# Q of a windowed attention transposed by DMA and read by the score matmuls as it lies, head by head on 64 rows

## Chip, cores, metric

One core of a Trainium2 chip. The sessions ran on different chips; the kernel before ran in each of them, with medians of 306.8 to 308.1 us, so times of different sessions are compared. The time is device microseconds of an execution; a number given for a kernel is the median of its runs. Ratios are the mean time of one kernel's fast runs over that of the other's fast runs of the same rounds, so they are not quite the ratio of the medians. A run more than 1.5% above the fastest of the same kernel counts as slow.

## The reference

```python
# q, k, v: 8 batches x 8 heads x 576 tokens x 64, values near 0.1; window of 64, causal
scores = q @ k.T / sqrt(64);  keep 0 <= i - j < 64;  attn = softmax(scores);  x = attn @ v
x = x.transpose(0, 2, 1, 3).reshape(4608, 512)
out = (((x @ w1) * (x @ w2)) @ w3) @ w_out          # 512 -> 1024 -> 1024 -> 512
```

The scores are so small that the softmax is nearly uniform over its window. An exchange of queries inside a batch need not be seen by the comparison with the reference.

## The kernel before

A batch has 6 steps, two for each third of 192 queries; a step covers two head pairs. K and Q of a batch are loaded as fp32 (576 tokens as 32 partitions x 18 tokens, for 4 head pairs), cast on POOL, transposed by DMA (at the start by PE), and put in token order by copies on ACT and DVE: K to `kT`, each of Q's two heads to its half of `qT`, whose other half is zero. One score matmul of 128 rows then serves both heads.

```python
    def load_qk(b, which, gate=None):
        ...
        for hh in range(2):
            nc.sync.dma_start(out=t[:, hh], in_=src[b, hh:H:2].rearrange("j (p r) d -> p j (r d)", r=TI))
    ...
    def scores(d):
        ...
                nc.tensor.matmul(s_ps[:, jj, c0:c0 + 2 * n].rearrange("k (a n) -> k a n", a=2),
                                 kT[:, 2 * jp + jj, k0:k0 + P], qT[:, 2 * jp + jj, :, q0:q0 + n], ...)
        nc.scalar.activation(pt[:, :, 0:w], s_ps[:, :, 0:w], AF.Exp, bias=-SHIFT, scale=scale)
        for (lo, hi, n, off, step) in ...:                      # masks, POOL, innermost 128 or 64
            nc.gpsimd.affine_select(out=sl, in_=sl, pattern=pat, compare_op=ALU.is_ge, fill=0.0, ...)
            nc.gpsimd.affine_select(out=sl, in_=sl, pattern=[[-s, m] for s, m in pat], ...)
    ...
    def values(d):
        o_ps = ps_v.tile([P, 2, 512], FP32, name="o_ps")        # one buffer only
        ...                                                     # matmuls, then ACT: Ln, Ln, Exp -> r
        nc.vector.tensor_tensor(xs[0:D], o_ps[0:D, :, 0:192], r[0:D], ALU.mult)
        nc.vector.tensor_tensor(xs[D:P], o_ps[D:P, :, 192:384], r[D:P], ALU.mult)
```

`xs` is a piece of `xT`, the fp16 input of the feed-forward part. V is loaded by casting loads that POOL issues; DVE copies halves of it (`copy_v`).

## Time and profile before

| | before |
|---|---|
| time | 307.23 us (306.78 to 309.35) |
| first scores in the trace | 15.9 us |
| busy PE / DVE / ACT / POOL | 269 / 214 / 191 / 195 us of 306 |
| from one batch's first scores to the next's, us | 39.5, 33.1, 29.9, 29.3, 31.9, 33.9, 27.4 |

The last row is worked out from the start times of the score matmuls. Groups of the profile: line, engine, operation, output and input with their shapes, count, then busy microseconds and mean ns of one, then the idle time before them.

### The profile page before, as it was taken

To read this page: it belongs to the slowest core of one execution; us is meant where nothing else is said; L and a number is where in the kernel's file an instruction comes from. 1 tells how busy PE (TensorE), PEld (TensorE's weight loads), DVE (VectorE), ACT (ScalarE), POOL (GpSimd) and SP (SyncE) were. 2 spreads that over 40 slices of the span, in tenths; PEclk is the share of its full clock that TensorE was granted. 3 is DMA by queue.
4 is the path that set the end of the run, shared out by engine and by line. 5 is a ranking of instruction groups with operands and counts; after the bars stand their busy time and mean duration, and the time that the engine had idled before them with its cause. 6 is when DMAs were issued, how large, how long until landed. Compare 5 with 4: busy or idle time off the path is not lost.

```text
span 306.0 us, 5153 instructions
## 1 busy us (share of the span) xinstructions
PE 269.2 (88%) x1846; PEld 154.0 (50%) x1846; DVE 213.8 (70%) x302; ACT 190.7 (62%) x296; POOL 194.7 (64%) x214
## 2 busy tenths in 40 slices
PE   8598989798477999997899689996999899999992
PEld 8584645444223455554455379553554455554440
DVE  6815687555977678887988877769799766455531
ACT  2423784686285959897689656497769865741310
POOL 9754994578617986899589835695888544320300
PEclk9869999999959999999999999999999999999998
DMA  6999999973774997599679945994179003003012
GB/s 245 203 183 199 299 237 247 351 48 85 183 196 112 320 97 215 89 326 105 164 133 301 113 136 113 330 163 80 23 144 130 0 25 116 0 6 136 0 39 106
DMA packets 79694, 45.88 MB, mean 150 GB/s; under 512 B 66816, under 2 KB 69888, under 8 KB 79664
## 3 DMA queue, kind: packets, MB, share of 16 engines
q0 software_dynamic: 41744, 9.96, 39.5%
q1 hardware_dynamic: 37920, 35.54, 38.9%
q8 instruction: 15, 0.25, 0.4%
q14 instruction: 15, 0.12, 0.2%
HBM read 38.80 MB, written 9.44 MB: 158 GB/s over the span
## 4 chain that ended last, share of the span: by engine, by line
PE 51%; DVE 12%; ACT 11%; issue 8%; DMA 8%; POOL 7%; SPq 1%; DVEq 0%; POOLq 0%; ACTq 0%
PE f_ps L416 24%; PE f_ps L429 12%; DMA v<-in_v_dram 5%; PE o_ps L329 5%; PE tp L500 4%; PE s_ps L294 3%; DVE xT L345 3%; POOL pt L308 3%; ACT qT L274 3%; ACT ln_s L339 2%; DMA stage<-in_q_dram 2%; ACT r L341 2%; DVE kT L274 2%; DVE t2k L431 2%; ACT pt L299 2%
## 5 line engine op out<-in xcount | busy, mean ns | idle before, releaser
L416 PE MATMUL f_ps<-xT,w_sb 128*128 128x512 f16 (+1 forms) x640 | 137.5, 361 | 11.7 <-DVE xT L345 4.4
L308 POOL TENSOR_SCALAR_AFFINE_SELECT pt<-pt 128x512 f16<-128x512 f16 (+1 forms) x64 | 61.2, 956 | 66.7 <-ACT pt L299 66.6
L416 PEld LDWEIGHTS <-w_sb 128*128 128x128 f16 x640 | 61.1, 98 | 65.6 <-issue 17.2
L429 PE MATMUL f_ps<-wc_sb,ab 128*128 128x512 f16 x288 | 67.2, 379 | 0.4
L422 DVE TENSOR_TENSOR ab<-f_ps,a_sb 128x512 f16<-128x512 f32 x72 | 49.5, 690 | 17.7 <-PE f_ps L416 14.6
L299 ACT ACTIVATE pt<-s_ps 128x1024 f16<-128x1024 f32 (+1 forms) x48 | 45.6, 950 | 23.4 <-PE s_ps L294 22.6
L310 POOL TENSOR_SCALAR_AFFINE_SELECT pt<-pt 128x512 f16<-128x512 f16 (+1 forms) x64 | 56.7, 885 | 4.4
L421 ACT COPY a_sb<-f_ps 128x512 f32<-128x512 f32 x72 | 41.5, 578 | 21.6 <-PE f_ps L416 21.4
L344 DVE TENSOR_TENSOR xT<-o_ps,r 64x384 f16<-64x384 f32 x48 | 26.3, 549 | 39.0 <-ACT r L341 38.6
L338 ACT ACTIVATE ln_s<-o_ps 64x384 f32<-64x384 f32 x48 | 23.4, 488 | 41.1 <-PE o_ps L329 40.9
L429 PEld LDWEIGHTS <-ab 128*128 128x128 f16 x288 | 27.5, 98 | 30.2 <-DVE ab L422 1.8
L329 PE MATMUL o_ps<-pt,v 128*128 128x128 f16 (+1 forms) x384 | 28.0, 215 | 11.4 <-DVE xT L345 7.3
L235 POOL DMA_DIRECT2D v<-in_v_dram x40 | 33.9, 855 | 5.4 <-DMA ab<-in_moe_w_out_dram 3.6
L329 PEld LDWEIGHTS <-v 128*128 128x128 f16 x384 | 23.6, 98 | 24.5 <-issue 11.0
L431 DVE COPY t2k<-f_ps 128x512 f32<-128x512 f32 x36 | 24.7, 689 | 9.4 <-PE f_ps L429 8.8
L294 PE MATMUL s_ps<-qT,kT 128*128 128x256 f16 x192 | 28.1, 271 | 2.2 <-ACT qT L274 2.2
L274 ACT COPY qT<-q_tr 64x768 f16<-64x768 f16 x18 | 27.5, 1536 | 3.2 <-DMA q_tr<-q 3.2
L345 DVE TENSOR_TENSOR xT<-o_ps,r 64x384 f16<-64x384 f32 x48 | 26.9, 561 | 0.6
L341 ACT ACTIVATE r<-ln_s 128x384 f32<-128x384 f32 x48 | 25.1, 523 | 1.5
L274 DVE COPY qT<-q_tr 64x768 f16<-64x768 f16 x18 | 23.7, 1323 | 0.5
L294 PEld LDWEIGHTS <-kT 128*128 128x128 f16 x192 | 18.0, 100 | 11.9 <-DVE qT L274 2.2
L339 ACT ACTIVATE ln_s<-o_ps 64x384 f32<-64x384 f32 x48 | 23.2, 483 | 0.6
(65 smaller groups left out, 189.5 us busy)
## 6 DMA issues: line engine op xcount, KB each, us to landing
stage<-in_k_dram SPq DMA_DIRECT2D x16, 576.0 KB
stage<-in_q_dram SPq DMA_DIRECT2D x16, 576.0 KB
out_dram<-t2k SPq DMA_DIRECT2D x36, 256.0 KB
v<-in_v_dram POOLq DMA_DIRECT2D x32, 128.0 KB, 8.3
w_sb<-in_moe_w_dram POOLq DMA_DIRECT2D x4, 512.0 KB, 9.3
ab<-in_moe_w_out_dram POOLq DMA_DIRECT2D x1, 1024.0 KB, 9.9
ab<-in_moe_w_dram POOLq DMA_DIRECT2D x2, 512.0 KB, 12.3
xT<-in_moe_w_dram POOLq DMA_DIRECT2D x2, 512.0 KB, 16.6
```

Source lines behind the costliest of these rows:

```text
L235: nc.gpsimd.dma_start(out=vh[lo:P, c], in_=v[b, :, s0:s0 + P - lo, :].rearrange("h s d -> s h d"))
L274: cp(dst[:, :, :, 6 * c:6 * c + 6], src[part])
L294: nc.tensor.matmul(s_ps[:, jj, c0:c0 + 2 * n].rearrange("k (a n) -> k a n", a=2), kT[:, 2 * jp + jj, k0:k0 + P], qT[:, 2 * jp + jj, :, q0: ...
L299: nc.scalar.activation(pt[:, :, 0:w], s_ps[:, :, 0:w], AF.Exp, bias=-SHIFT, scale=scale)
L308: nc.gpsimd.affine_select(out=sl, in_=sl, pattern=pat, compare_op=ALU.is_ge, fill=0.0, base=off, channel_multiplier=-1)
L310: nc.gpsimd.affine_select(out=sl, in_=sl, pattern=[[-s, m] for s, m in pat], compare_op=ALU.is_ge, fill=0.0, base=63 - off, channel_multip ...
L329: nc.tensor.matmul(o_ps[:, jj, o0:o0 + n], v16[:, si * 2 + bi, j0 + jj, a * D:a * D + P], pt[:, jj, c0 + a * n:c0 + a * n + n], start=firs ...
L345: nc.vector.tensor_tensor(xs[D:P], o_ps[D:P, :, 192:384], r[D:P], ALU.mult)
L416: nc.tensor.matmul(d[:, f * n + c0:f * n + c1], w[:, dc, (fc + f) * P:(fc + f + 1) * P], xT[:, dc, xc:xc + c1 - c0], start=first, stop=(dc ...
L421: act_cp(a_sb[:, 0:nf * n], a_ps[:, 0:nf * n])
L422: nc.vector.tensor_tensor(ab[:, fc:fc + nf, lo:hi], b_ps[:, 0:nf * n].rearrange("p (f n) -> p f n", f=nf), a_sb[:, 0:nf * n].rearrange("p ...
L429: nc.tensor.matmul(o_ps, ab[:, fc, t * P:t * P + P], wc_sb[:, fc, :], start=(fc == 0), stop=(fc == 7))
```

## The change

The intent: K must still be put in order, but Q need not. The DMA's transposed tile is read as it lies, so 24 copies on each of ACT and DVE go, and so do the zero halves. The queries now come in the order (i, p), where token = 16 p + i, and each head has its own matmul on 64 rows. To make runs of 16 tokens fit, 512 tokens of a batch are loaded as 32 x 16 with the head pairs outermost, and the last 64 tokens of all batches come in one extra load. The products must then put the tokens back.

```diff
-    qTs = [const.tile([P, NJ, 2, S], FP16, name=f"qT_{i}") for i in range(2)]
+    qlast = const.tile([P, QI, P], FP16)
...
+                nc.sync.dma_start(out=t[:, hh, 0:QI * D],
+                                  in_=q[b, hh:H:2, 0:TP * QI].rearrange("j (p r) d -> j p (r d)", r=QI))
...
+                for a in range(2):
+                    half = slice(a * D, a * D + D)
+                    rhs = qT[half, :, TP * j + p0:TP * j + p0 + np] if p0 < TP else \
+                        qlast[half, :, 16 * b + 4 * j:16 * b + 4 * j + np]
+                    nc.tensor.matmul(s_ps[:, a, jj, c0:c0 + QI * np].rearrange("k (i p) -> k i p", i=QI),
+                                     kT[half, j, k0:k0 + P], rhs, start=True, stop=True, skip_group_check=True)
...
-                pat = [[0, 2], [step, nb], [0, 2], [1, n]]
+                pat = [[0, 4], [step, nb], [1, QI], [QI, np]]          # np = 8 or 4
...
-        nc.vector.tensor_tensor(xs[0:D], o_ps[0:D, :, 0:192], r[0:D], ALU.mult)
+        xs = xs.rearrange("m j (p i) -> m j i p", i=QI)
+        for a in range(2):
+            half = slice(a * D, a * D + D)
+            nc.vector.tensor_tensor(xs[half],
+                                    o_ps[half, :, a * 192:a * 192 + 192].rearrange("m j (i p) -> m j i p", i=QI),
+                                    r[half].rearrange("m j (i p) -> m j i p", i=QI), ALU.mult)
...                                                                    # start: PE transposed Q of batches 0 and 1 before
+    cast_qk(0, "q", 0, dve_cp)
+    cast_qk(0, "q", 1, act_cp)
+    turn(0, "q")
+    load_qk("last", "q")
```

## The prediction

> **What bounds the kernel now.** I began with the page's busy shares and its 40 slices.
>
> ```profile
> PE 269.2 (88%) x1846; PEld 154.0 (50%) x1846; DVE 213.8 (70%) x302; ACT 190.7 (62%) x296; POOL 194.7 (64%) x214
> ...
> PE   8598989798477999997899689996999899999992
> ...
> POOL 9754994578617986899589835695888544320300
> ```
>
> PE is the bound on average, but it dips in slices 10 to 12 (71 to 91 us of 306), and POOL is at 8 or 9 tenths in several slices up to the 30th. In the busy times by stretch POOL has 25.3 of 30 us in 110 to 140 and 24.9 in the next 30, while PE has 29.9 and 26.8: POOL is the second bound, with little to spare there. The list of waits says what POOL's reserve is, and the chain of work that ended last shows the dip:
>
> ```profile
> POOL pt L308 <- ACT pt L299: 66.6, 25, 8.4
> ```
>
> ```profile
> 85.19 2.65 SPq L252
> 87.89 0.59 SPq L208
> 88.53 6.75 DMA stage<-in_q_dram
> 95.33 1.15 POOL q L216
> 96.47 0.60 POOL pt L308
> ```
>
> 66.6 us is nearly all the time in which POOL waits for work between its first mask and its last. The chain near 90 us runs over a load of Q: POOL, strictly in order, waits in its cast for the load, and the masks stand behind the cast. The groups by shape give what the change removes:
>
> ```profile
> L274 ACT COPY qT<-q_tr 64x768 f16<-64x768 f16 x18 | 27.5, 1536 | 3.2 <-DMA q_tr<-q 3.2
> ...
> L294 PE MATMUL s_ps<-qT,kT 128*128 128x256 f16 x160 | 27.0, 278 | 2.2 <-ACT qT L274 2.2
> ...
> L274 DVE COPY qT<-q_tr 64x768 f16<-64x768 f16 x18 | 23.7, 1323 | 0.5
> ```
>
> Those 51 us of copies are large, but the waits they end are small: 3.2 us on ACT, 2.2 on PE. Last, the timeline of POOL, undisturbed masks:
>
> ```profile
> 1.17 0.29 POOL masks.py:199 TENSOR_SCALAR_AFFINE_SELECT ident<-ident 128x128 f16<-128x128 f16 x1
> ...
> 20.23 0.65 POOL L308 TENSOR_SCALAR_AFFINE_SELECT pt<-pt 128x512 f16<-128x512 f16 x1
> 20.95 0.64 POOL L310 TENSOR_SCALAR_AFFINE_SELECT pt<-pt 128x512 f16<-128x512 f16 x1
> 21.55 0.42 POOL L308 TENSOR_SCALAR_AFFINE_SELECT pt<-pt 128x256 f16<-128x256 f16 x1
> ...
> 31.37 1.12 POOL L310 TENSOR_SCALAR_AFFINE_SELECT pt<-pt 128x1024 f16<-128x1024 f16 x1
> ```
>
> **What the Trainium skill says.** (1) "DMA: Bandwidth & Descriptors", section "Why a DMA increments its semaphore by 16 and not by 1": a DMA runs on the largest k up to 16 that divides the slowest dimension of both sides. Every Q and K load of before has slowest dimensions 32 (source) and 128 (tile), so k = 16; its packets confirm it, with 14.2 in flight on average in the first four loads (2.4 to 9.6 us). (2) "GPSIMD Engine Reference", 3.1: a software loop with a body of up to two operations costs 1.03 cycles per element at 1.2 GHz, 0.86 ns. The trace agrees: its records have 418, 639 and 1,115 ns for undisturbed masks of 256, 512 and 1,024 elements; 639 - 418 = 221 ns over 256 elements is 0.86 ns. (3) "TensorEngine Tiling (Array Packing)", Key Properties: tiles on different rows can run in parallel, and a change of tiling mode drains TensorE. Before has one mode in its matmuls of note, so nothing shows it. (4) "Advanced Engine Details and Errata", Memory Cachelines: access that leaves a line each time is penalized. The trace agrees for SBUF: ACT's 768-element copy takes 1,536 ns from the strided transposed tile and about 800 from PSUM.
>
> **The change part by part.**
>
> *Removed.* ACT: 24 copies to qT, 27.5 + 4.8 (six from PSUM of 0.80) = 32 us. DVE: 24, 23.7 + 5.7 (six of 0.96) = 29 us, and four memsets, 4.1 us, all before 6.2 us when DVE waits for K anyway. PE: 36 transposes of Q, some 2 us, and the waits near 50 us (49.8 to 54.5) in which they, ACT and DVE took turns: 2 to 3 us of path. In the steady batches I give the freed ACT and DVE time 2 to 4 us of path, because PE seldom waits for them.
>
> *Scores and values on PE.* Per score step 4 matmuls of mostly 256 columns on 128 rows become 8 or 12 of 128 or 64 columns on 64 rows (192 to 448 in all). The columns stay 1,024, some 0.44 us in the timeline (start to start of the next group). If the two halves run in parallel it is 0.22 us, at most 48 x 0.22 = 10 us saved; two changes of mode a step, which I guess at 0.1 us each, eat 48 x 0.2 = 10. Values keep their columns (384 to 448 matmuls; the 64-column ones cost about 30 ns start to start) but write PSUM in runs of 4 or 8, point (4). I take PE as neutral, within 5 us. DVE's write of xT, now in steps of 16, may lose part of what DVE gained.
>
> *Masks.* Elements stay equal, instructions go from 128 to 160 (the last third of a batch needs two pairs). But the innermost dimension of the mask's pattern falls from 128 or 64 to 8 or 4. Rows of a pattern per batch before: 4 steps' instructions, 16 each with 4 rows in the first third's two steps (8 instructions, 32 rows) and 8 instructions of 8 rows (64), so 96. After: first third 2 x 4 x 64 = 512, second 2 x 2 x 128 = 512, last 2 x (2 x 64 + 2 x 128) = 768, so 1,792. What a row costs the trace shows only weakly. Take 0.863 ns per element off: 183 ns stay for the identity's mask (1 row), 197 for 256 and 512 elements (4 rows), 232 for 1,024 (8 rows). That is 4.3 ns a row from 1 to 4 and 8.8 from 4 to 8; the mean slope is 49 / 7 = 7 ns, as a software loop that restarts per row would have. Then POOL gains 8 batches x 1,696 rows x 7 ns = 95 us, and 32 instructions x 0.17 = 5 us; casts of Q, 1,152 to 1,024 elements, give back 13 x 0.11 = 1.4 us. POOL's busy time between the first mask (20.2 us) and the last (ends 269.7) is 177 us, so it becomes about 275, more than the 250 us that this stretch now takes: POOL becomes the bound.
>
> *Loads of Q.* The new order puts the four head pairs outermost in the source: slowest dimensions 4 and 128, so k = 4 by point (1). A 4,608-byte packet takes 178 ns in the trace, so one of 4,096 some 158 (estimate); 256 packets on 4 engines are 64 x 158 ns = 10.1 us, where the pair of K and Q loads now lands in 7.2 us together. At the start Q follows K on the same rings, from about 5.5 us, shares its engines with the weights from 8.6 us, and lands near 17 instead of 9.6. Then the casts (1 us) and the transpose: the first one of before was issued at 73.4 and its packets ended at 77.6, so 4.2 us. First scores at about 23 us instead of 15.9; the filler matmuls end near 15.6, so the clock falls and the next 40 fillers run slower, 1 us more. First mask about 25 us. For batch 1, Q lands 6 to 8 us later than its cast is due (now 42.3 and 43.9), another 5 us, less the 3 saved there; at the dip, the load alone takes 10 us instead of 6, another 4. Later loads have 20 us from issue to cast (129.7 and 151.9) and stay hidden.
>
> *Sum.* First mask 25 + POOL's work 275 + 20 us in which it still has none (start, batch 1, the dip) + the tail after the last mask, now 306.0 - 269.7 = 36, partly taken forward by PE's reserve, say 32: 352 us.
>
> **The rivals.** *Rows cost nothing* (the 35 ns between 4 and 8 rows is a matter of 1,024 elements): POOL gains only 5 us, and the time is 307 + 7 to 8 (start) + 2 (batch 1) + 4 (dip) - 6 (copies, scores) = about 314. For it: a straight line through the four durations misses none by over 7 ns. Against: both steps in the rest, 1 to 4 rows and 4 to 8, go up. *The load stays on 16 engines*, and POOL is free as well: start about equal (transpose lands at 16), 4 to 10 us gained, 297 to 303. For it: the filler count of 110 fits a first score at 15.6. Against: the skill's rule is explicit, and Q's order before obeyed it. *PE gets worse*: drains of 0.3 us and slow strided writes would add 48 x 0.5 = 24 us where PE is the bound, 335 with rows free, and hidden behind POOL otherwise. *POOL far worse*: at 12 ns a row 163 us instead of 95, 420.
>
> **Range and chances.** I give a row cost of 4 to 10 ns seven chances in ten: 4 ns leaves POOL just below its bound and makes some 315 to 328 with the loads' terms, 10 ns about 393. Range 312 to 395, middle 352. Faster by over 2% (under 301) needs free rows, 16 engines and overlapping scores: 0.06. Within 2%: 0.09. Slower: 0.85.
>
> **What would show it.** Right: a 512-element mask near 1.1 us instead of 0.64 and a 1,024-element one near 2 instead of 1.12; POOL over 80% busy, PE below 80%; PE's waits for POOL's pt at L308 in tens of us where it is 3.2 now; POOL's wait for ACT shrunk; Q's first load landing after 15 us and the first scores after 20. Wrong: masks of unchanged length, or first scores near 16 us, each of which takes its term out of the sum.

## More of the kernel before

```profile
L345 DVE TENSOR_TENSOR xT<-o_ps,r 64x384 f16<-64x384 f32 x48 | 26.9, 561 | 0.6
L344 DVE TENSOR_TENSOR xT<-o_ps,r 64x384 f16<-64x384 f32 x48 | 26.3, 549 | 39.0 <-ACT r L341 38.6
```

These are the 96 products, 53 us on DVE, 0.55 us each. They read `o_ps`, and until both are done the next step's values cannot start.

## The result

454.85 us (450.99 to 460.12, 4 runs); before 307.34 in the same rounds; ratio 1.474, 95% interval 1.462 to 1.486. The result is right. The direction was predicted, the size was not: 352 was predicted, at most 395. The profile is of the slowest run, 458.3 us of span, which counts as slow (2.0% above the fastest); the three others are 451 to 455, and nothing below rests on that difference. Times read from its trace are some 5 us longer than the median.

The page of the changed kernel, busy times and three of the rows of 40 slices:

```profile
PE 306.9 (67%) x2215; PEld 158.3 (35%) x2215; DVE 298.1 (65%) x274; ACT 163.8 (36%) x273; POOL 299.7 (65%) x246
...
PE   8200665596765809678657765969677768767994
...
DVE  2000167882688545498959996878789897865642
...
POOL 9110469926985449949995999459969977654020
```

PE fell from 88% to 67%, as "PE below 80%" said, but POOL is at 65%, not over 80%: no engine is the bound. POOL is all but idle in slices 2 to 4 (11 to 46 us), where it had work before, and DVE, hardly discussed in the prediction, is as busy as POOL and stays at 8 or 9 tenths over long stretches.

The masks came out as predicted. Timeline of POOL in the changed kernel (start us, us of duration, instruction; in brackets the idle time before it):

```profile
51.49 1.09 POOL L306 TENSOR_SCALAR_AFFINE_SELECT pt<-pt 128x512 f16<-128x512 f16 x1 [24.15 <-ACT pt L295]
...
53.71 0.89 POOL L306 TENSOR_SCALAR_AFFINE_SELECT pt<-pt 128x256 f16<-128x256 f16 x1
...
64.72 2.08 POOL L306 TENSOR_SCALAR_AFFINE_SELECT pt<-pt 128x1024 f16<-128x1024 f16 x1 [3.66 <-ACT pt L295]
```

1.09 us where 0.64 stood for 512 elements, 2.08 where 1.12 stood for 1,024, as announced ("near 1.1", "near 2"). But the first mask comes at 51.5 us (before 20.2), after 24 us of waiting. The products did not come out as predicted. Group of the changed kernel:

```profile
L344 DVE TENSOR_TENSOR xT<-o_ps,r 64x384 f16<-64x384 f32 x96 | 171.8, 1789 | 48.9 <-ACT r L338 48.0
```

The same 96 products, 1,789 ns each instead of 549 and 561: 119 us more on DVE. The list of waits of the changed kernel (waiting instruction, releaser, us in total, times, longest) says where that shows:

```profile
POOL pt L306 <- ACT pt L295: 94.4, 21, 24.1
...
PE o_ps L326 <- DVE xT L344: 49.2, 25, 6.6
...
PE o_ps L326 <- POOL pt L308: 15.7, 6, 9.7
```

The same wait for the products in the kernel before:

```profile
PE o_ps L329 <- DVE xT L345: 7.3, 9, 2.1
```

PE waits 49 us for the products, where it was 7, and less than half of that for the masks, and POOL still waits 94 us for work. A step with little else in it shows the loop: values at 61.70 us, ACT's Ln, Ln, Exp until 63.73, the two products from 63.77 for 3.57 us, the next values at 67.49, so 5.8 us a step. In the kernel before the values of the same stretch start at 30.50 and 33.88, 3.4 us apart.

Last, the start. Chain of waits of the changed kernel, cut off at 50 us (start us, us, what):

```profile
3.03 18.84 DMA stage<-in_q_dram
...
21.89 1.05 ACT q L218
...
22.96 10.62 SPq L252
...
34.27 15.30 DMA stage<-in_q_dram
```

Q's first load takes until 21.9 us (before: 9.6), the transposition's issue alone takes 10.6 us, its packets run from 26.9 to 46.1 us, and the first scores are at 47.2 us instead of 15.9. The last line of the chain is the load of the last 64 tokens of all batches: its cast stands on ACT in front of the first exp, which starts at 50.6 us although the first scores were there at 47.7. TensorE had nothing to do from 14.8 us to the first scores, and its granted clock was 0.50 from 20 us on.

The differences can be laid out along the trace, always from first scores to first scores of the next batch. Of 458.3 - 306.0 = 152 us, 31 are in the start (47.2 - 15.9), 104 in the seven intervals (58.1, 46.7, 51.9, 43.1, 44.6, 46.7, 38.2, sum 329, before 225), and 17 from the last batch's first scores to the end (81.9, before 65.1).

### The profile page after: what moved, and what is told of

Same layout as the page of the kernel before. It is cut to its first block, busy times and chain, and to the rows that moved or that the text cites. A ratio compares the mean times of both kernels' runs of the same rounds, so it can differ in the third digit from the quotient of the medians.

```text
span 458.3 us, 5881 instructions
## 1 busy us (share of the span) xinstructions
PE 306.9 (67%) x2215; PEld 158.3 (35%) x2215; DVE 298.1 (65%) x274; ACT 163.8 (36%) x273; POOL 299.7 (65%) x246
## 4 chain that ended last, share of the span: by engine, by line
DMA 27%; PE 20%; DVE 16%; issue 14%; POOL 12%; ACT 6%; SPq 4%; DVEq 0%; ACTq 0%; POOLq 0%
DMA stage<-in_q_dram 15%; PE f_ps L416 11%; DVE xT L344 9%; DMA v<-in_v_dram 9%; POOL pt L306 5%; PE f_ps L429 4%; SPq L252 3%; DMA q_tr<-q 3%; PE o_ps L326 3%; POOL pt L308 3%; POOL v L236 2%; DVE t2k L431 2%; ACT r L338 2%; ACT ln_s L336 2%; DVE ab L422 2%
## 5 line engine op out<-in xcount | busy, mean ns | idle before, releaser
L344 DVE TENSOR_TENSOR xT<-o_ps,r 64x384 f16<-64x384 f32 x96 | 171.8, 1789 | 48.9 <-ACT r L338 48.0
L306 POOL TENSOR_SCALAR_AFFINE_SELECT pt<-pt 128x512 f16<-128x512 f16 (+1 forms) x80 | 112.8, 1409 | 94.5 <-ACT pt L295 94.4
L416 PE MATMUL f_ps<-xT,w_sb 128*128 128x512 f16 (+1 forms) x640 | 156.9, 400 | 25.2 <-DVE ab L422 15.6
L308 POOL TENSOR_SCALAR_AFFINE_SELECT pt<-pt 128x512 f16<-128x512 f16 (+1 forms) x80 | 112.4, 1405 | 5.5
L416 PEld LDWEIGHTS <-w_sb 128*128 128x128 f16 x640 | 65.6, 107 | 92.8 <-issue 47.2
L326 PE MATMUL o_ps<-pt,v 128*128 128x128 f16 (+1 forms) x448 | 31.2, 219 | 71.5 <-DVE xT L344 49.2
L429 PE MATMUL f_ps<-wc_sb,ab 128*128 128x512 f16 x288 | 71.2, 396 | 9.9 <-DVE ab L422 7.4
L295 ACT ACTIVATE pt<-s_ps 128x1024 f16<-128x1024 f32 (+1 forms) x48 | 45.5, 949 | 32.7 <-PE s_ps L291 31.2
L326 PEld LDWEIGHTS <-v 128*128 128x128 f16 x448 | 25.7, 103 | 91.1 <-issue 84.9
L291 PE MATMUL s_ps<-q_tr,kT 64*128 64x128 f16 (+1 forms) x384 | 19.6, 223 | 37.1 <-DMA q_tr<-q 34.5
L429 PEld LDWEIGHTS <-ab 128*128 128x128 f16 x288 | 27.6, 100 | 42.6 <-issue 13.3
L291 PEld LDWEIGHTS <-kT 64*128 64x128 f16 x448 | 12.7, 100 | 55.8 <-issue 54.3
L431 DVE COPY t2k<-f_ps 128x512 f32<-128x512 f32 x36 | 23.8, 687 | 8.0 <-PE f_ps L429 7.6
L268 DVE COPY kT<-k_tr 128x768 f16<-128x768 f16 x18 | 22.8, 1272 | 2.7 <-DMA k_tr<-k 2.5
L240 DVE COPY v<-v 64x512 f16<-64x512 f16 x16 | 9.6, 601 | 18.5 <-DMA v<-in_v_dram 18.2
```

The source lines that it names most:

```text
L295: nc.scalar.activation(pt[:, :, :, 0:w], s_ps[:, :, :, 0:w], AF.Exp, bias=-SHIFT, scale=scale)
L326: nc.tensor.matmul(o[:, :, p0 - QP * si:p0 - QP * si + np], v16[:, VBLK.index(k0), j0 + jj, a * D:a * D + P], pt[:, a, jj, c0:c0 + QI * np ...
L344: nc.vector.tensor_tensor(xs[half], o_ps[half, :, a * 192:a * 192 + 192].rearrange("m j (i p) -> m j i p", i=QI), r[half].rearrange("m j ( ...
L416: nc.tensor.matmul(d[:, f * n + c0:f * n + c1], w[:, dc, (fc + f) * P:(fc + f + 1) * P], xT[:, dc, xc:xc + c1 - c0], start=first, stop=(dc ...
L429: nc.tensor.matmul(o_ps, ab[:, fc, t * P:t * P + P], wc_sb[:, fc, :], start=(fc == 0), stop=(fc == 7))
L431: dve_cp(o_sb, o_ps)
```

## The experiments

The theory: three things cost time, the products' store (S), the masks' rows (M), and Q's loads on 4 engines with the slow transposition at the start (L). Rivals: contention lengthens the records (then the operations alone would be as fast as before), or matmuls on 64 rows with short runs cost PE what the profile does not show. All kernels that write tokens or queries in another order give a wrong result on purpose.

### The disputed costs alone

A kernel of its own: four 64 x 384 products each from PSUM, with the output in steps of 1, 2, 4, 8 and 16 elements, as in the change, and with the step on the inputs instead; masks with 4, 16, 64 and 128 rows; Q's load with 4 and with 32 outermost; a transposition alone and beside two loads that cast; score matmuls with operands in different orders.

```diff
+    perm = x16[H, 0:384].rearrange("m (j p i) -> m j i p", j=2, i=16)
+    for _ in range(4):                                                      # as in the change (L117)
+        nc.vector.tensor_tensor(perm, ip.rearrange("m j (i p) -> m j i p", i=16),
+                                rr.rearrange("m j (i p) -> m j i p", i=16), ALU.mult)
```

> The disputed costs by themselves; its output is zeros on purpose. Theory (three separate prices): the product into xT, 64 x 384, costs about 0.55 us when its fp16 output is contiguous and about 1.75 us in the change's order, and the same rise comes with a plain step of 16 elements (32 bytes), without the permutation; at steps of 2 and 4 elements it is clearly less. Read in permuted order and written in a row it stays under 0.8 us. A 512-element mask takes 0.64, about 0.73, 1.09 and 1.55 us with 4, 16, 64 and 128 rows (7.5 ns a row). Q's load takes about 10 us with 4 outermost in the source and about 3 us with 32. The transpose takes about 4 us alone and over 8 beside loads that cast. Rival A: the write costs 1.75 us only because POOL or DMA work beside it, so all orders of it are near 0.55 us here. Rival B: the row cost of the mask is contention too, so all masks take 0.64 us. For the matmuls nothing is claimed: 64-row pairs as they lie 27 to 55 ns a matmul start to start; runs of 8 the same; read 256 bytes apart between the same and four times that.

Timeline of DVE, with output steps of 1, 4, 8 and 16 elements in the first four lines, fp32 output in a row and at steps of 8 elements in the next two, the change's order in the seventh, and the step on the inputs in the last:

```profile
48.30 2.30 DVE L102 TENSOR_TENSOR x<-o_ps,r 64x384 f16<-64x384 f32 x4 [25.77 <-PE o_ps L92]
...
53.08 4.11 DVE L106 TENSOR_TENSOR x<-o_ps,r 64x384 f16<-64x384 f32 x4
57.22 7.51 DVE L108 TENSOR_TENSOR x<-o_ps,r 64x384 f16<-64x384 f32 x4
64.76 7.11 DVE L110 TENSOR_TENSOR x<-o_ps,r 64x384 f16<-64x384 f32 x4
71.53 2.47 DVE L112 TENSOR_TENSOR x<-o_ps,r 64x384 f32<-64x384 f32 x4
74.04 3.45 DVE L114 TENSOR_TENSOR x<-o_ps,r 64x384 f32<-64x384 f32 x4
77.34 7.11 DVE L117 TENSOR_TENSOR x<-o_ps,r 64x384 f16<-64x384 f32 x4
84.49 3.32 DVE L119 TENSOR_TENSOR x<-o_ps,r 64x384 f16<-64x384 f32 x4
```

Without any contention the product in the change's order takes 1.78 us, in a row 0.575, three times as much, and the whole of it is the output's step: with the inputs stepped and the output in a row it is 0.83. A step of 2 elements costs nothing (2.41 us for four), 4 elements 1.8 times, from 8 on three times. The step in bytes alone does not decide: fp32 output at steps of 8 elements, 32 bytes, takes 1.4 times as long as in a row (3.45 and 2.47), where fp16 at the same 32 bytes takes 3.1 times. An ACT copy shows the same, 0.50 and 1.78 us. A mask of 512 elements takes 637 ns with 4 rows, 719 with 16, 1,087 with 64, 1,633 with 128: 6.8 to 8.5 ns a row. Q's load took 11.7 us with 4 outermost (3.8 packets in flight) and 4.6 with 32 (12.0 in flight); this is the rule of "DMA: Bandwidth & Descriptors" that the prediction cites. The transposition's packets took 2.6 us alone (23.8 to 26.4 us, after an issue at 22.6), and 11.6 us (33.9 to 45.5, after an issue at 29.6) beside two casting loads. A pair of score matmuls on the two halves runs 28 ns a matmul start to start, in a row or in runs of 8 (56 ns a pair, as long as one matmul on 128 rows with the same 128 columns at the same granted clock of 1.0), and 108 to 112 when single queries lie 256 bytes apart, so the change's own order was the cheap one for PE. The contention rival falls; the operations are slow by themselves.

### One of the three undone at a time

S: the products to `xT` in a row.

```diff
-        xs = xs.rearrange("m j (p i) -> m j i p", i=QI)
...
+            nc.vector.tensor_tensor(xs[half], o_ps[half, :, a * 192:a * 192 + 192], r[half], ALU.mult)
```

> The change, with xT written in the order in which the sums lie (wrong columns, so a wrong result on purpose); nothing else differs. Theory: the write in steps of 32 bytes holds the single o_ps buffer, so a step of values takes 5.8 us where it took 3.4; without it the products take 0.55 us, DVE loses 118 us of busy time and the time falls by 70 to 95 us, to 360 to 385, where POOL's masks bound it. Rival (the prediction's: POOL is the bound already): the time falls by less than 15 us, to 440 or more.

Measured 416.96 us, ratio to before 1.349 (1.340 to 1.358): 38 us gained, less than I expected.

M: the masks' patterns with long rows.

```diff
-                pat = [[0, 4], [step, nb], [1, QI], [QI, np]]
+                pat = [[0, 4], [step, nb], [1, QI * np]]
```

> The change, with the masks' patterns in long rows (inner dimension 128 or 64; the mask is then in another order than the queries, a wrong result on purpose), same count of masks and elements. Theory: POOL's masks fall from 1.09 to 0.64 us and from 2.08 to 1.12, some 95 us of POOL, but the time falls by only 5 to 25 us, because DVE's write stays in the loop: 430 to 450. Rival (POOL is the bound): 60 us or more less, under 395.

Measured 441.54 us, ratio 1.434 (1.424 to 1.443): 13 us gained, though POOL's busy time fell from 300 to 190 us.

L: Q's loads with 32 outermost, for 16 engines.

```diff
-                                  in_=q[b, hh:H:2, 0:TP * QI].rearrange("j (p r) d -> j p (r d)", r=QI))
+                                  in_=q[b, hh:H:2, 0:TP * QI].rearrange("j (p r) d -> p j (r d)", r=QI))
```

> The change, with Q's loads in the order of before, 32 outermost (columns of other queries, a wrong result on purpose). Theory: Q's first load lands at 9 to 11 us instead of 21.4, POOL's waits for Q (8 us) and batch 1's wait vanish, the time falls by 12 to 30 us, to 425 to 443; the first transpose still takes far over 4 us because it runs beside the loads of the weights. Rival (the loads are hidden but for the start): 10 to 12 us less.

Measured 412.86 us, ratio 1.336 (1.329 to 1.344): 42 us gained, more than expected. First scores at 25.5 us, still 10 later than before. (Its queries are exchanged between heads.) The three gains sum to 93 of 148 us. Either something else costs 55, or the three hide one another.

### All three undone, and single ones put into the kernel before

All three edits above together:

> The change with all three suspects taken out together (products written to xT in a row, masks in long rows, Q's loads in a layout that 16 engines can take; wrong result on purpose: the queries come out in another order). Theory (the three cover for one another, and nothing else of the change costs much): the three single gains, 38 + 13 + 42 = 93 us, are far less than the whole: 315 to 330 us, with the first scores still near 29 us as in the run with 16 engines alone (12 us later than before), and POOL near 200 us busy. Rival (the matmuls on 64 rows with short strided runs cost PE some 40 to 60 us, which the profile hides): 350 us or more, with PE over 85% busy.

Measured 312.73 us, ratio 1.017 (1.011 to 1.023). So nothing else of the change costs much, and the rival of PE's 64-row matmuls falls: in this trace the score matmuls of a step start within 0.15 to 0.25 us, before within 0.27 to 0.33 with three exceptions. PE is busy for 272.5 us, before 269.2, at a granted clock of 0.96, before 0.97. So the 307 busy us of the change, at a clock of 0.86, go with its waits and not with the form of its matmuls.

The store alone, in the kernel before:

```diff
+        xs = xs.rearrange("m j (p i) -> m j i p", i=16)                     # and both inputs alike
```

> The kernel before with one thing of the change: the products are written to xT in steps of 16 elements (wrong result on purpose: tokens in another order). DVE gets 96 x 1.2 = 115 us more to do. Theory (each step's product is in the loop over the one o_ps buffer, and DVE goes from 214 to about 330 us busy): 375 to 430 us. Rival (the prediction's: DVE has room, the stores are mostly hidden): 310 to 335 us.

Measured 398.75 us, ratio 1.300 (1.293 to 1.307). The page and the group:

```profile
PE 291.9 (74%) x1846; PEld 160.1 (40%) x1846; DVE 320.2 (81%) x302; ACT 191.6 (48%) x296; POOL 191.1 (48%) x214
...
L347 DVE TENSOR_TENSOR xT<-o_ps,r 64x384 f16<-64x384 f32 x96 | 172.3, 1795 | 31.1 <-ACT r L341 29.8
```

One line of the kernel, 91 us; DVE is the busiest engine at 81%.

The masks' rows alone, in the kernel before (the masks' meaning is lost, their work kept):

```diff
-                pat = [[0, 2], [step, nb], [0, 2], [1, n]]
+                off = 0
+                pat = [[0, 8], [1, 16], [16, 8]]
```

> The kernel before with one thing of the change: masks' patterns with an innermost length of 8 or 4 (1,440 more rows a batch, 8 x 1,440 x 7.5 ns = 86 us more on POOL, from 195 to about 280 us; wrong result on purpose). Theory and the prediction agree here: POOL becomes the bound, 330 to 365 us, with PE's waits for POOL's pt in tens of us. Rival (POOL's reserve of 67 us takes most of it): 308 to 325 us.

Measured 351.87 us, ratio 1.145 (1.139 to 1.151). Its page and its waits:

```profile
PE 288.3 (82%) x1846; PEld 161.5 (46%) x1846; DVE 222.7 (64%) x302; ACT 191.0 (55%) x296; POOL 283.9 (81%) x214
```

```profile
PE o_ps L330 <- POOL pt L311: 33.6, 20, 3.2
```

POOL at 81%, PE's wait for `pt` at 33.6 us: this is the picture that the prediction drew for the whole change, and it is right for the masks alone. That the time is also the predicted one is luck: the prediction's 352 us contain a first mask 5 us later than before and 20 us without work for POOL, mostly for the loads, which this run does not have. In its terms this run is 20.9 + 266.2 + 28.1 + 35.0 = 350.2 us of span; by the prediction's way of counting, with the first mask as before and no time without work, the masks alone would have made some 315 us.

The loads alone, in the change with S and M undone:

> The change with the products in a row and the masks in long rows (both undone, wrong result on purpose), so that of the three costs only the loads of Q on 4 engines and what follows at the start remain; to be read against the run with all three undone (312.7 us). Theory (the load's late arrival costs at the start and in the first batches, where nothing is there to hide it, but not later, where loads are asked for 20 us ahead): first scores near 46 us, 345 to 370 us. Rival 1 (the prediction's sizes: 8 + 2 + 4 us): 320 to 330 us. Rival 2 (each load of each batch comes too late): 385 us or more, with gaps of PE at every batch.

Measured 399.82 us, ratio 1.299 (1.289 to 1.309), 87 us more than with all three undone. That is the number of rival 2 (the reason will turn out to be another), and far from the prediction's 14 to 20.

How they hide one another shows when the intervals from batch to batch are put side by side (worked out as in the table of before):

| | to first scores | intervals between batches, us |
|---|---|---|
| before | 15.9 | 39.5, 33.1, 29.9, 29.3, 31.9, 33.9, 27.4 |
| before + S | 15.9 | 54.5, 45.2, 37.4, 38.0, 40.3, 46.9, 35.9 |
| before + M | 16.0 | 47.7, 41.3, 36.0, 33.7, 39.4, 36.6, 33.7 |
| change with L only | 42.6 | 54.6, 30.1, 55.0, 44.7, 39.9, 41.0, 25.7 |
| largest of these three | | 54.6, 45.2, 55.0, 44.7, 40.3, 46.9, 35.9 |
| the change | 47.2 | 58.1, 46.7, 51.9, 43.1, 44.6, 46.7, 38.2 |
| all three undone | 25.2 | 46.4, 31.4, 29.4, 27.3, 29.0, 31.7, 25.7 |

In each batch the change takes about as long as the largest of the three alone (sum 322.6, measured 329.3). So undoing one helps only down to the next, and the three single gains must fall short of the whole. The runs with one cost undone test this: the largest of the two that are left gives 310 us for the seven intervals without S, 323 without M and 298 without L, and their traces have 305, 315 and 303. The agreement is arithmetic, but these three runs do not enter the table. The end belongs to S: from the last batch's first scores it takes 81.9 us in the kernel before with S, 65.9 with M, and 65.2 in the change with S undone.

### Where the loads' 87 us are

Transposition at the start: Q of batches 0 and 1 and the last rows turned by PE into PSUM and copied without a reordering, all else as with the three undone.

```diff
-    turn(0, "q")
+    for c in range(3):
+        cast_part(0, c, act_cp if c == 1 else dve_cp)
+    turn_pe(0, [tps[3], ps_t.tile([P, 6, P], FP16, name="tp"), spare(ps_s, "s_ps")[0]], [act_cp, dve_cp, act_cp])
```

> As the run with all three undone (312.7 us), and Q of batches 0 and 1 and the last rows transposed on PE, with plain copies, as the kernel before did at its start (wrong result on purpose). Theory (what was left of the loss at the start is the transposition by DMA beside the weights' loads, 10 to 12 us, and the one of batch 1, 12 us on the chain): first scores at 16 to 18 us, 288 to 300 us, that is faster than before. Rival (the weights' loads take their time in any case, and the start is moved, not shortened): 305 to 315 us.

Measured 295.58 us, ratio 0.965 (0.958 to 0.971); first scores at 14.1 us. The transposition by DMA of batches 0 and 1 and of the last rows, with what stood around it, cost the 17 us that come on top of the 87: 11 of them before the first scores. The edit also shortens the fillers (110 and 30 matmuls become 25 and 15) and moves the casts of the last rows behind the first two scores; these were not tried apart.

Then 4 engines for Q from batch 2 on only, and the same without V's loads from batch 2 on (these batches use the V that is there).

```diff
+                                      "j (p r) d -> p j (r d)" if b < 2 else "j (p r) d -> j p (r d)", r=QI))
```

> As the run with the start on PE and nothing else of the three costs (295.6 us), but Q's loads from batch 2 on in the change's layout, on 4 engines (wrong result on purpose). Theory (the later loads are not hidden: they slow V's loads, which DVE's copies wait for, 8 to 15 us a batch in five batches): 335 to 365 us, DVE's wait for V in tens of us. Rival (the 87 us are the start and batch 1, the later loads are hidden as predicted): 296 to 310 us.

Measured 359.85 us, ratio 1.170 (1.160 to 1.180): 64 us for loads that the prediction held for hidden. That leaves 23 of the 87 us to the loads of batches 0 and 1 (first scores at 42.6 us against 25.2); no run has these alone. Chain of this run, and DVE's timeline at the same place:

```profile
151.76 1.76 POOL v L237 x2
153.52 22.86 DMA v<-in_v_dram
...
178.60 1.01 PE o_ps L344 x12
```

```profile
157.14 0.69 DVE L446 COPY t2k<-f_ps 128x512 f32<-128x512 f32 x1
176.41 0.29 DVE L241 COPY v<-v 64x512 f16<-64x512 f16 x1 [18.58 <-DMA v<-in_v_dram]
```

It is V that arrives late. Q's packets of that batch run from 152.4 to 169.3 us, 3.7 in flight, and V's, issued at the same time, from 153.6 to 177.1; in the kernel before, V's of a batch took 7 to 8 us in the later batches. DVE waits 18.6 us in a copy of V, and the products stand behind it. The list of waits has it as a total:

```profile
DVE v L241 <- DMA v<-in_v_dram: 62.0, 5, 18.6
```

4.7 us in the kernel before. A wait shows only what came last, hence the last run:

```diff
     def load_v(b, *blocks):
+        if b >= 2:
+            return
```

> As the run with later loads on 4 engines, with V's loads of batches 2 and later left out (those batches use the V that is there; wrong result on purpose). Theory (V's loads carry the loss): back to 292 to 305 us, though Q's loads still take 12 us or more each. Rival (Q itself comes too late, V's wait only stood in front of it): within 12 us of the run with V's loads.

Measured 303.95 us, ratio 0.989 (0.981 to 0.997). Q's loads still take 11 to 14 us each there, on 4 engines. So 56 of the 64 us go by way of V. The rest is 8 us; one interval of this run is 12 us longer than without any of the three (40.3 against 28.6 us), and POOL waits 12 us in all for a late Q. V's absence also leaves the DMA engines less to do, which the run cannot tell from the wait itself.

### Ways to keep the change

The right result without S: the step on the product's inputs.

```diff
-        xs = xs.rearrange("m j (p i) -> m j i p", i=QI)
+        xs = xs.rearrange("m j (p i) -> m j p i", i=QI)                     # inputs "m j (i p) -> m j p i"
```

> The change with the same product, but written in xT's own order, and PSUM and r read with a step instead (right result). By the measured costs alone (0.83 us a product in place of 1.78, where one without any step is 0.58) the step loop of the values is 1.9 us shorter a step than in the change and 0.5 us longer than in the run with xT in a row (417.0 us): theory 418 to 430 us. Rival (a strided read from PSUM costs as much as a strided write, in the full kernel): 445 us or more.

427.13 us, 417.14 to 428.02; three of its four runs, the profiled one too, count as slow against the fourth, so the gain over the change (27 to 38 us) is not sharp. A product took 0.82 us in the trace.

Two versions with a right result leave the ordering to ACT's exp, which reads the scores from PSUM with a step and writes them in token order, so that masks, values and products stay as before the change; Q of batches 0 and 1 and the last rows is turned by PE. In the first, one load for each head pair keeps Q's layout (in batch 0, ACT issues half of them); in the second, one load in K's layout (p outermost) makes the score matmuls read Q at steps of 8 bytes.

```diff
+        pt = sb.tile([P, 4, 256], FP16, name="pt", bufs=3)
+        nc.scalar.activation(pt[:, :, 0:w].rearrange("k f (p i) -> k f p i", i=QI),
+                             s_ps.rearrange("k a j n -> k (a j) n")[:, :, 0:w].rearrange("k f (i p) -> k f p i", i=QI),
+                             AF.Exp, bias=-SHIFT, scale=scale)
```

> A version meant to be right and fast: Q is still read by the scores as it lies, one load per head pair (32 outermost on both sides, so 16 engines), ACT's exp reads the scores from PSUM with a step and writes them in natural order, so that masks, values and the products stay as they were before the change; Q of batches 0, 1 and the last rows transposed by PE. Theory (ACT loses at most 0.45 us a step, 20 us in all, of which it saves 27 on copies, and the order costs nothing elsewhere): 285 to 303 us, right result. Rival (the step of 64 bytes in PSUM doubles or triples exp, or the scores' short runs in PSUM slow PE): 310 us or more.

315.25 us, ratio 1.027 (1.021 to 1.033), right result, not the 285 to 303 expected. From batch 1 on the median time of its Q packets was 250 to 309 ns, load by load, where those of whole-tile loads take 159 to 172, and its V waits are 16.4 us; why they are longer was not tried.

> As the version with the order in exp, but each half of Q comes by one load in K's layout (32 outermost too), so the scores read Q at steps of 4 elements (8 bytes) in place of runs. Theory (reading at a step of 8 bytes costs PE up to the factor of 4 that a step of 256 bytes cost, 0.33 us a step become up to 1.3): equal to the other version within 2% if 8 bytes are free, up to 15 us slower if not.

300.70 us (300.02 to 302.15), ratio 0.980 (0.975 to 0.985), right result: faster than both kernels, though whether by over 2% the interval leaves open, and 15 us faster than the other version, which neither side of the expectation had. Groups of the kernel before, then of this one:

```profile
L299 ACT ACTIVATE pt<-s_ps 128x1024 f16<-128x1024 f32 x32 | 32.6, 1019 | 12.8 <-PE s_ps L294 12.4 <-POOL pt L310 0.2
```

```profile
L316 ACT ACTIVATE pt<-s_ps 128x1024 f16<-128x1024 f32 x32 | 32.6, 1018 | 17.6 <-PE s_ps L312 16.9 <-POOL pt L328 0.8
```

The exp that reorders costs exactly what the plain one does. The steps of 8 bytes cost PE some: a step's score matmuls start within 0.26 to 0.36 us, with runs within 0.15 to 0.22, so about 0.12 x 48 = 6 us, an estimate that would cover the distance of 5 us to the version that ignores the order (295.6).

## Why the prediction was wrong

Its sum was 25 + 275 + 20 + 32 = 352 us. Read from the trace in the same terms:

| term | predicted | measured | off by |
|---|---|---|---|
| first mask | 25 | 51.5 | +26.5 |
| POOL's work from first to last mask (51 to 420 us) | 275 | 282 | +7 |
| POOL without work between them | 20 | 84 | +64 |
| after the last mask | 32 | 41 | +9 |
| sum | 352 | 458.5 | +106.5 |

- *Masks: right in price.* 7 ns a row were predicted from a weak difference in the profile (one slope in it is misworked: 197 - 183 ns over 3 rows are 4.7 ns, not 4.3; the sum does not use it), 6.8 to 8.5 measured; what makes the cost is not shown. POOL rose by 105 us, from 195 to 300, where 95 + 5 - 1.4 = 99 were predicted. Masks alone cost 45 us of time, and their 351.9 us agree with the predicted sum by luck, as said above. The rival "rows cost nothing" falls.
- *The step that failed first: "DVE's write of xT, now in steps of 16, may lose part of what DVE gained."* DVE had gained 29 us of copies. The write cost 119 us in the change and 91 us of time by itself. There was a warning: the prediction cites "Advanced Engine Details and Errata", Memory Cachelines, and finds an ACT copy of 1,536 ns from SBUF that takes 800 from PSUM. This does not size a step, as both copies read with the same step of 128 elements, and no strided fp16 write stood in the trace. But a factor of 2 on the products would have been 53 us more, in the loop over the one `o_ps` buffer. I counted rows of the masks to the unit and left this one at "may".
- *"Later loads have 20 us from issue to cast and stay hidden": wrong.* The casts wait for them little (8 us in the change), but V's loads start beside them, take 17 to 25 us instead of 7 or 8, and DVE's copies of V stop the products: 64 us for the loads from batch 2 on, 56 of them by way of V, in the runs in which nothing else is slow. In the change itself, where each batch takes longer anyway, V's later loads took 12 to 16 us and DVE waited 18 us for them. The rule of 4 engines was applied rightly, and the neighbour on the same engines forgotten.
- *"The transposes took 4.2 us": taken from an undisturbed one.* At the start it runs beside the weights' loads: an issue of 10.6 us, packets for 19 us. Q itself came at 21.1 us where I had put it near 17. First scores 47.2 us, predicted 23.
- *"POOL becomes the bound": wrong, although its work was right.* With the products and V in the way it has 84 us without work. That the masks, S and L lie over one another fits the intervals and explains how 45, 91 and 87 us alone make 148 together. So the direction was right, but mostly through two costs that the prediction had small: with the masks' rows undone the change is still 1.434 times as long.
- *PE neutral: right* (272.5 us busy with all three undone, 269.2 before), and pairs on 64 rows do run in parallel: a step's score matmuls start within 0.15 to 0.25 us against mostly 0.27 to 0.33, in agreement with "TensorEngine Tiling (Array Packing)", Key Properties, that tiles on different rows can. No drain of note showed.

What stays open: why the loads for single head pairs have longer packets, whether the transposition is slow beside the weights' loads for their bytes or because they cast, and how the loads of batches 0 and 1 divide their 23 us.

## What to carry to other kernels

When a layout step is dropped, write down for each access that becomes strided its factor and the loop it stands in, first of all for writes of 2-byte values, before any row of a pattern is counted. A transfer that has time to spare is not hidden if it crowds out a neighbour on the same DMA engines that somebody waits for. And put a reordering where the run shows it to be free, here in the exp that reads PSUM.

## What the Trainium skill lacked or had wrong

- "Advanced Engine Details and Errata", Memory Cachelines, speaks of a penalty without a size. Measured for fp16 output of a 64 x 384 product on DVE: step of 2 elements 1.05 times, 4 elements 1.8, 8 elements 3.3, 16 elements 3.1; fp32 output at 8 elements 1.4; an ACT copy to fp16 3.6 times at 16.
- "GPSIMD Engine Reference", 3.1, counts cycles per element and a fixed part per instruction, nothing per row of the pattern. A mask's pattern costs besides 6.8 to 8.5 ns a row (637 ns with 4 rows, 1,633 with 128, for the same 512 elements).
- "DMA: Bandwidth & Descriptors", Rules for kernel authors, says of order that "A transpose next to ordinary DMAs needs nothing". That is about order and right results; the page has no figure for the time beside other loads: packets over 2.6 us alone, 11.6 beside two casting loads, 19 at the start of the changed kernel.
- The same page's rule of k, in the section on the semaphore, held (11.7 us on 4 engines, 4.6 on 16); what is lacking is a figure for the effect on others: V's loads beside such a load took 17 to 25 us in place of 7 to 8.
- "PSUM — Partial Sum Buffer", Specifications, says that any non-contiguous access pattern "slows matmuls significantly". Scores written to PSUM in runs of 8 took 220 ns a matmul (order in exp, a load per head pair), as in a row (220, start on PE), so not any pattern does; single elements apart were not tried. Exp, of which that line does not speak, read PSUM at steps of 64 bytes in 1,018 ns against 1,019. A moving operand read from SBUF at steps of 256 bytes did slow matmuls, from 28 to about 110 ns start to start.
